# Value weights streamed in whole rows, and the segment's output turned into columns in two parts

## The chip, the cores and the metric

The kernel runs on one core of a Trainium2 chip. The metric is the device time of one execution in microseconds, as the median over several runs; lower is better. Four kinds of engine matter here: TensorE (PE, with PEld for its weight loads), VectorE (DVE), ScalarE (ACT) and GpSimd (POOL). SyncE (SP) issues most of the DMA transfers, and 16 DMA engines carry them.

## What is computed

The reference is a stack of four layers, A, B, A, B, each added to its input after a normalisation of the rows. Layer A is the one that matters here: attention in segments with a recurrent memory. The 2048 rows are cut into 64 segments of 32 rows. Eight rows of memory go in front of each segment, and the first eight rows of a segment's output are the memory of the next, so the segments can't run side by side.

```python
mem = mem0                                    # 8 rows of 640
for s in range(64):
    h = concatenate([mem, x[32*s:32*s+32]])   # 40 rows of 640
    q, k, v = h @ Wq, h @ Wk, h @ Wv          # 32 heads of 192
    p = softmax(where(mask, q @ k.T * scale, -1e9))
    o = (p @ v) @ Wo                          # back to 640 columns
    mem = o[:8]; outs.append(o[8:])
```

All inputs are in bf16. Wq, Wk and Wv are 640 x 6144 each, Wo is 6144 x 640. Layer B is a linear attention over all rows at once; the change doesn't touch it.

## The kernel before

Layer A has a part that is done for all segments at once (`A_pre`) and a chain over the 64 segments (`A_chain`), whose order on every engine is the order in which the program is written (`manual_schedule`). The last eight rows of each segment are projected in `A_pre`; the chain itself handles 32 rows: eight of memory and the segment's first 24. They lie in `hT` as columns: 128 partitions x 5 blocks x 32 columns, where block b holds every fifth one of the 640 features and the first eight columns of a block are the memory.

**A segment in rounds.** The 32 heads go in four rounds of eight. A round projects Q, K and V (`project`, L885: five blocks of four matmuls each), copies Q and K to SBUF on ACT (`to_raw`, L895), turns them on DVE (`to_rows`, L900 and L903 to L905), takes scores (`scores`, L922 and L927), exponentials and sums, weighs the values (`attend`, L935), and multiplies by the round's rows of Wo into one PSUM bank `W` (`wo_round`, L961), which gathers all four rounds. The order of the rounds turns round from segment to segment, so that the last round of one is the first of the next.

**Streamed weights.** Not all weights fit into SBUF. For each of Q, K and V, three of the five blocks (blocks 2, 3 and 4) of rounds 0 and 3 share a slot. In the first round of each segment `project` takes these three blocks first (its order of blocks is 2, 3, 4, 0, 1), and after each block `load_slot` issues on SP's queue the load of the last round's weights into that slot. Q comes as one DMA per block, whole rows of 3072 B in each of 128 partitions; K and V come as two DMAs per block, half rows of 1536 B. After the first round's `wo_round`, `load_wo` loads Wo's rows of the last round from `wo_rows` in six DMAs of 320 KB. So SP issues 21 weight loads in each segment, in this order: three of Q, six of K, six of V, six of Wo. A DMA on SP's queue waits for the DMA issued eight before it, since the framework has eight semaphores for this queue.

**The end of a segment.** After the last `wo_round` (with `keep_busy` and `fill`, which give PE matmuls and weight loads whose results nobody uses), the bank `W` holds the segment's output rows. DVE turns its 160 columns in 32 x 32 blocks into the tile `wt` (L1101) and copies eight columns of each of the five blocks into `hT` in bf16 (L1102). With that the next segment's first projection, Q of round 0, may start. After these, `keep_tail` (L949, L950) and `keep_rows` (L849, four ACT copies from `W`) put away what belongs to the output. In `W` an access by one engine waits for the other engines' earlier ones, reads included: that is how the framework orders the accesses to one PSUM bank.

Of the kernel before, what the change touches and what calls it, by code (L numbers as in the profile page):

```python
# [115 lines left out]
class Kernel:  # L116
# [456 lines left out]
    def layer_A(self, xn_dram, at_dram, li, x_raw=None):  # L573
        nc, tc = self.nc, self.tc
        KC, NSEG = self.KC, self.NSEG
        dram = self.dram
        NR = 4
        PW = 1536
        self.kqb_d = dram.tile([NSEG, P, NR, 192], BF16, name=f"kqb{li}")
        self.vb_d = dram.tile([NSEG, NR, 2, 8, 896], BF16, name=f"vb{li}")  # L580
        self.otb_d = dram.tile([NSEG, P, 384], BF16, name=f"otb{li}")
        wview = self.wview
        wov = self.A_Wo.rearrange("h d m -> (h d) m").rearrange("(c p) m -> p c m", p=P)
        low = self.view(0, LATE)
        at = LATE
        res, slot = {}, {}
        for r in (3, 2):
            for m in "KQV":
                for b in range(KC - (SLOTS[m] if r == 3 else 0)):
                    res[m, r, b] = low[:, len(res) * PW:len(res) * PW + PW]  # L590
        assert len(res) * PW * 2 == LATE
        for m, r, b in [(m, 0, b) for m in "KQV" for b in range(KC - SLOTS[m])] + \
                [(m, None, b) for m in "KQV" for b in range(KC - SLOTS[m], KC)] + [(m, 1, b) for m in "KQV" for b in range(KC)]:
            v = self.view(at, 2 * PW)
            at += 2 * PW
            if r is None:
                slot[m, b] = v
            else:
                res[m, r, b] = v
        holds = {}  # L600
        wo_mid = self.view(at, 24 * 1280)
        wo_end = self.view(at + 24 * 1280, 12 * 1280)
        assert at + 36 * 1280 == ARENA
        unread = set(res)

        def load_slot(m, r, b, whole=False):
            if holds.get((m, b)) != r:
                holds[m, b] = r
                w = PW if whole or m == "Q" else PW // 2
                for h in range(0, PW, w):  # L610
                    nc.sync.dma_start(out=slot[m, b][:, h:h + w], in_=wview[m][:, b, PW * r + h:PW * r + h + w])

        def load_matrix(m, r):
            for b in range(KC):
                if (m, r, b) in unread:
                    unread.remove((m, r, b))
                    nc.sync.dma_start(out=res[m, r, b], in_=wview[m][:, b, PW * r:PW * r + PW])
                elif (m, r, b) not in res:
                    load_slot(m, r, b, True)

        early = {(0, 5), (2, 4), (2, 5), (1, 0), (1, 1), (1, 2), (1, 3)}

        def load_wo(r, into=None, part=range(6)):
            t = into if into is not None else wo_end[:, :] if r in (0, 3) else wo_mid[:, 7680 * (r - 1):7680 * r]
            for k in part:
                tk = t[:, 1280 * k:1280 * k + 1280]
                if r in (0, 3):
                    self.last_load = nc.sync.dma_start(out=tk, in_=self.wo_rows[r // 3, :, 1280 * k:1280 * k + 1280])
                else:
                    nc.sync.dma_start(out=tk.rearrange("p (c m) -> p c m", m=640),  # L630
                                      in_=wov[:, 12 * r + 2 * k:12 * r + 2 * k + 2, :])

        def piece(m, r, b):
            assert (m, r, b) in res or holds[m, b] == r
            return res[m, r, b] if (m, r, b) in res else slot[m, b]

        def lay_out_wo():
            if li == 0:
                self.wo_rows = dram.tile([2, P, 7680], BF16, name="wo_rows")
                for i, r in enumerate((0, 3)):  # L640
                    nc.scalar.dma_start(out=self.wo_rows[i].rearrange("p (c m) -> p c m", m=640),
                                        in_=wov[:, 12 * r:12 * r + 12, :])

        def early_wo():
            for r in (0, 2, 1):
                load_wo(r, part=[k for k in range(6) if (r, k) in early])

        def late_wo(r):
            load_wo(r, part=[k for k in range(6) if (r, k) not in early])

        self.A_pre(xn_dram, li, load_matrix, piece, wo_mid, wo_end, lay_out_wo, early_wo, x_raw)
        self.A_chain(xn_dram, at_dram, li, load_slot, piece, load_wo, late_wo, wo_mid, wo_end, low)
        self.post_args = at_dram, wo_mid, wo_end, low

# [159 lines left out]
    def A_chain(self, xn_dram, at_dram, li, load_slot, piece, load_wo, late_wo, wo_mid, wo_end, low):  # L814
        nc, tc, KC, NSEG = self.nc, self.tc, self.KC, self.NSEG
        scale = float(self.Dh) ** -0.5
        NR = 4
        with tc.tile_pool(name=f"A{li}_ch", reuse_waits="tile", bufs=1) as sp, \
# [25 lines left out]
            def new_hT():  # L844
                return sp.tile([P, KC, 32], BF16, name="hT", tag="hT")
# [98 lines left out]
            def keep_tail(o, late=False):  # L944
                otb = sp.tile([P, 6, 16], BF16, name="otb", tag="otb", bufs=2)
                if late:
                    nc.vector.tensor_copy(out=otb[:, 0:3, :], in_=o[0][:, :, 64:80])
                else:
                    nc.scalar.activation(out=otb[:, 0:3, :], in_=o[0][:, :, 64:80], func=ACT.Copy)  # L949
                nc.vector.tensor_copy(out=otb[:, 3:6, :], in_=o[1][:, :, 64:80])  # L950
                return otb

            def store_tail(otb, s, r):
                nc.gpsimd.dma_start(out=self.otb_d[s, :, 96 * r:96 * r + 96], in_=otb[:, :, :].rearrange("p c t -> p (c t)"))  # L954
# [56 lines left out]
            hT = new_hT()  # L1011
            hx_transpose(hT, range(4))
            load_rows(1)
            for s in range(NSEG):
                W = pop.tile([P, 512], F32, name="ps_w", tag="w")
# [67 lines left out]
                if s + 1 < NSEG:  # L1083
                    hT = new_hT()
# [13 lines left out]
                fill(SEG_FILL)  # L1098
                if s + 1 < NSEG:
                    wt = sp.tile([P, KC, 32], F32, name="wt", tag="raw")  # L1100
                    nc.vector.transpose(out=wt[:, :, :], in_=W[:, 0:160].rearrange("p (j b) -> p b j", b=KC))  # L1101
                    nc.vector.tensor_copy(out=hT[:, :, 0:8], in_=wt[:, :, 0:8])  # L1102
                store_tail(keep_tail(o), s, order[L])
                keep_rows(W)
            store_rows(NSEG - 1)
# [66 lines left out]
```

## Time and profile before

| What | Value |
|---|---|
| Median of 6 runs | 3784.98 us (3777.33 to 3793.9) |
| The profiled execution | 3787.65 us, of which its span 3785.9 us |
| Mean granted TensorE clock | 0.976 |
| PE / PEld / DVE / ACT / POOL busy | 94% / 61% / 62% / 55% / 44% |
| Bytes read from HBM, written | 855.97 MB, 72.09 MB |
| First and last transpose at a segment's end (L1101), first layer A | 250.1 and about 1578 us |
| The same, second layer A | 2122.9 and 3444.9 us |

The busy share of PE is a mean over the span. In the rows of groups, the columns are: line, engine, operation, output and inputs with their shapes and the count; then busy time and the mean duration of one; then the engine's idle time just before these instructions and what ended it. In the timeline the columns are the start, the duration, the engine, the line, the operation, the tiles and the count, and in brackets the idle time before it with its releaser.

### The profile page before, as it was taken

To read this page: it belongs to the slowest core of one execution; us is meant where nothing else is said; L and a number is where in the kernel's file an instruction comes from. 1 tells how busy PE (TensorE), PEld (TensorE's weight loads), DVE (VectorE), ACT (ScalarE), POOL (GpSimd) and SP (SyncE) were. 2 spreads that over 40 slices of the span, in tenths; PEclk is the share of its full clock that TensorE was granted. 3 is DMA by queue.
4 is the path that set the end of the run, shared out by engine and by line. 5 is a ranking of instruction groups with operands and counts; after the bars stand their busy time and mean duration, and the time that the engine had idled before them with its cause. 6 is when DMAs were issued, how large, how long until landed. Compare 5 with 4: busy or idle time off the path is not lost. (4 is left out here: it accounts for less than half of the span.)

```text
span 3785.9 us, 169628 instructions
## 1 busy us (share of the span) xinstructions
PE 3546.5 (94%) x71080; PEld 2324.9 (61%) x71408; DVE 2329.1 (62%) x6038; ACT 2074.5 (55%) x5285; POOL 1671.4 (44%) x4367
## 2 busy tenths in 40 slices
PE   7889999999999999889899899999999999999898
PEld 5666666666666666545468566666666666665453
DVE  3546666666666666645643566666666666664565
ACT  2246666655666666536432566665666666664553
POOL 2435555545555555430242455545555555554300
PEclk9999999999999999989899999999999999999899
DMA  9788888887888888840377888888788888889100
GB/s 325 238 266 280 278 286 274 292 273 270 293 279 287 288 284 291 295 145 1 121 241 202 293 283 287 287 282 279 274 292 282 288 287 275 289 277 314 54 1 28
DMA packets 587913, 935.32 MB, mean 247 GB/s; under 512 B 147322, under 2 KB 402826, under 8 KB 587146
## 3 DMA queue, kind: packets, MB, share of 16 engines
q1 hardware_dynamic: 449194, 805.76, 61.2%
q0 software_dynamic: 68288, 88.95, 7.8%
q10 hardware_dynamic: 69664, 29.76, 3.0%
q8 instruction: 558, 9.14, 1.0%
q14 instruction: 209, 1.71, 0.1%
HBM read 855.97 MB, written 72.09 MB: 245 GB/s over the span
## 5 line engine op out<-in xcount | busy, mean ns | idle before, releaser
L885 PE MATMUL ps_qk<-arena,hT 128*32 128x384 bf16 x20480 | 1003.8, 328 | 28.5 <-DMA arena<-in_A_Wk_dram 6.9
L885 PEld LDWEIGHTS <-hT 128*32 128x32 bf16 x30720 | 741.2, 96 | 447.2 <-DVE hT L1102 33.5
L895 ACT ACTIVATE raw<-ps_qk 128x384 bf16<-128x384 f32 x1024 | 502.9, 491 | 445.8 <-PE ps_s L993 250.4
L961 PE MATMUL ps_w<-arena,OT 128*32 128x160 bf16 x24576 | 542.5, 234 | 27.0 <-DMA arena<-wo_rows 24.2
L868 POOL DMA_DIRECT2D Vp<-vb x512 | 259.5, 507 | 655.6 <-PE ps_o L935 452.2
L885 PE MATMUL ps_v<-arena,hT 128*32 128x384 bf16 x10240 | 536.3, 330 | 0.0
L961 PEld LDWEIGHTS <-OT 128*32 128x32 bf16 x24576 | 435.4, 97 | 120.9 <-issue 42.1
L900 DVE STREAM_TRANSPOSE KT<-raw 128x384 bf16<-128x384 bf16 x512 | 296.1, 578 | 201.5 <-ACT raw L895 197.5
L903 DVE STREAM_TRANSPOSE QT<-raw 128x256 bf16<-128x256 bf16 x512 | 228.0, 445 | 266.8 <-ACT raw L895 239.0
L856 POOL DMA_DIRECT2D kqb<-kqb x512 | 291.1, 569 | 165.7 <-POOL KT L864 148.4
L916 DVE CAST Vp<-ps_v 64x384 bf16<-64x384 f32 x512 | 286.1, 559 | 89.8 <-ACT Vp L914 75.6
L954 POOL DMA_DIRECT2D otb<-otb x512 | 283.5, 554 | 107.3 <-DVE otb L950 68.8
L914 ACT ACTIVATE Vp<-ps_v 64x384 bf16<-64x384 f32 x512 | 246.3, 481 | 144.6 <-PE ps_v L885 107.8
L941 DVE CAST OT<-ps_o 128x192 bf16<-128x192 f32 x512 | 183.1, 358 | 209.5 <-PE ps_o L935 192.8
L1000 DVE TENSOR_TENSOR E<-E,ps_s 80x320 bf16<-80x320 bf16 x512 | 247.4, 483 | 73.5 <-ACT ps_s L999 69.5
L935 PEld LDWEIGHTS <-Vp 80*128 80x128 bf16 x4096 | 181.5, 99 | 172.1 <-issue 124.0
L979 ACT ACTIVATE E<-ps_s 80x320 bf16<-80x320 f32 x512 | 221.9, 433 | 112.1 <-PE ps_s L927 99.6
L935 PE MATMUL ps_o<-E,Vp 80*128 80x80 bf16 x4096 | 234.0, 202 | 31.8 <-DMA Vp<-vb 8.6
L927 PE MATMUL ps_s<-QT,KT 128*80 128x80 bf16 (+1 forms) x3072 | 234.5, 214 | 24.0 <-DVE KT L900 15.3
L861 POOL COPY QT<-kqb 128x64 bf16<-128x64 bf16 x512 | 126.4, 247 | 281.6 <-PE ps_s L927 278.9
L927 PEld LDWEIGHTS <-KT 128*80 128x80 bf16 x3072 | 206.7, 120 | 55.6 <-issue 45.1
L940 ACT ACTIVATE OT<-ps_o 128x192 bf16<-128x192 f32 x512 | 167.9, 328 | 129.5 <-PE ps_o L935 129.3
(148 smaller groups left out, 5458.7 us busy)
## 6 DMA issues: line engine op xcount, KB each, us to landing
arena<-wo_rows SPq DMA_DIRECT2D x792, 320.0 KB, 6.0
arena<-in_A_Wq_dram SPq DMA_DIRECT2D x430, 384.0 KB, 4.6
arena<-in_A_Wk_dram SPq DMA_DIRECT2D x768, 192.0 KB, 4.7
arena<-in_A_Wv_dram SPq DMA_DIRECT2D x768, 192.0 KB, 5.4
kqb<-arena ACTq DMA_DIRECT2D x16, 1536.0 KB, 8.7
kqb<-kqb POOLq DMA_DIRECT2D x512, 48.0 KB, 5.0
arena<-in_A_Wk_dram SPq DMA_DIRECT2D x46, 384.0 KB, 7.1
arena<-in_A_Wv_dram SPq DMA_DIRECT2D x46, 384.0 KB, 7.8
```

Source lines behind the costliest of these rows:

```text
L856: nc.gpsimd.dma_start(out=kqb[:], in_=self.kqb_d[s, :, r, :])
L868: nc.gpsimd.dma_start(out=Vs[n % 2][64:80, :], in_=self.vb_d[s, r].rearrange("g t f -> (g t) f"))
L885: nc.tensor.matmul(o[32 * g:32 * g + 32, 0:384], lhsT=hT[:, b, :], rhs=rhs, start=(i == 0), stop=(i == KC - 1), tile_position=(0, 32 * g), ...
L895: nc.scalar.activation(out=raw[:], in_=ps[:, 0:384], func=ACT.Copy)
L900: nc.vector.transpose(out=KT[:, :, 0:64], in_=raw[:, :].rearrange("p (c j) -> p c j", j=64))
L914: nc.scalar.activation(out=o, in_=i, func=ACT.Copy)
L916: nc.vector.tensor_copy(out=o, in_=i)
L927: nc.tensor.matmul(S[0:80, c0:c0 + 80 * (q1 - q0)], lhsT=KT[:, 3 * x + i, :], rhs=QT[:, x, q0:q1, :], start=False, stop=(x == 1 and i == 2 ...
L935: nc.tensor.matmul(O[x][:, 80 * i:80 * i + 80], lhsT=Vs[n % 2][0:80, 448 * x + k:448 * x + k + 128], rhs=E[0:80, 160 * x + 80 * e:160 * x ...
L954: nc.gpsimd.dma_start(out=self.otb_d[s, :, 96 * r:96 * r + 96], in_=otb[:, :, :].rearrange("p c t -> p (c t)"))
L961: nc.tensor.matmul(W[32 * g:32 * g + 32, 0:160], lhsT=OT[:, c, q:q + 32], rhs=w[:, 640 * i + 160 * g:640 * i + 160 * g + 160], start=(firs ...
L1000: nc.vector.tensor_tensor(out=E[0:80, 0:320], in0=E[0:80, 0:320], in1=rc, op=ALU.mult)
```

## The change

Two edits. `load_slot` now loads V in one DMA per block with whole rows of 3072 B, as it does Q; K stays in halves. At the segment's end, DVE turns and copies blocks 2, 3 and 4 first (96 columns), and then blocks 0 and 1 (64 columns): four instructions in place of two.

```diff
         def load_slot(m, r, b, whole=False):
             if holds.get((m, b)) != r:
                 holds[m, b] = r
-                w = PW if whole or m == "Q" else PW // 2
+                w = PW if whole or m in "QV" else PW // 2
                 for h in range(0, PW, w):
                     nc.sync.dma_start(out=slot[m, b][:, h:h + w], in_=wview[m][:, b, PW * r + h:PW * r + h + w])
...
                 if s + 1 < NSEG:
                     wt = sp.tile([P, KC, 32], F32, name="wt", tag="raw")
-                    nc.vector.transpose(out=wt[:, :, :], in_=W[:, 0:160].rearrange("p (j b) -> p b j", b=KC))
-                    nc.vector.tensor_copy(out=hT[:, :, 0:8], in_=wt[:, :, 0:8])
+                    for b0, b1 in ((2, 5), (0, 2)):
+                        nc.vector.transpose(out=wt[:, b0:b1, :], in_=W[:, 0:160].rearrange("p (j b) -> p b j", b=KC)[:, b0:b1, :])
+                        nc.vector.tensor_copy(out=hT[:, b0:b1, 0:8], in_=wt[:, b0:b1, 0:8])
                 store_tail(keep_tail(o), s, order[L])
                 keep_rows(W)
```

## The prediction

> **What bounds the kernel now.** I read the page first: PE is busy nearly everywhere, but the DMA engines are too, and the bulk of it is SP's queue, q1.
>
> ```profile
> PE 3546.5 (94%) x71080; PEld 2324.9 (61%) x71408; DVE 2329.1 (62%) x6038; ACT 2074.5 (55%) x5285; POOL 1671.4 (44%) x4367
> ...
> DMA  9788888887888888840377888888788888889100
> ...
> q1 hardware_dynamic: 449194, 805.76, 61.2%
> ...
> L961 PE MATMUL ps_w<-arena,OT 128*32 128x160 bf16 x24576 | 542.5, 234 | 27.0 <-DMA arena<-wo_rows 24.2
> ...
> arena<-in_A_Wq_dram SPq DMA_DIRECT2D x430, 384.0 KB, 4.6
> ...
> arena<-in_A_Wv_dram SPq DMA_DIRECT2D x768, 192.0 KB, 5.4
> ```
>
> So I cut one segment (1006.08 to 1027.68, from L1101 to L1101) into windows. Columns: stretch, length, busy time of PE, PEld, DVE, ACT, POOL, clock, DMA share, GB/s.
>
> ```profile
> 1006.08:1008.00 1.92, 1.77 (x37) 1.16 (x40) 0.64 (x3) 1.43 (x5) 0.00 (x0) 1.00 0.05 11
> 1008.00:1016.00 8.00, 7.91 (x180) 4.82 (x172) 6.14 (x16) 5.23 (x14) 4.90 (x14) 1.00 1.00 349
> 1016.00:1025.00 9.00, 8.84 (x256) 5.95 (x244) 6.01 (x16) 5.95 (x16) 4.96 (x14) 1.00 0.97 335
> 1025.00:1027.68 2.68, 2.11 (x63) 1.67 (x64) 1.59 (x5) 0.54 (x2) 1.61 (x3) 1.00 0.32 95
> ```
>
> For 17 us the DMA engines are full; at both ends they are idle. Setting the record of landings against the starts of L1101 shows what that means. The 124 intervals between two L1101 (62 in each layer A) sum to 2649.8 us: the shortest is 20.84, the median 21.21. In 63 of them the next L1101 comes 0.41 us (within 0.025) after the segment's last Wo piece lands: they hold 36.7 us over 20.85 each. In the others PE's own work is the bound, plus scattered stalls. Two chains run side by side, then: PE's order, about 20.85 us, and the transfers, which start behind the first Q matmuls and end with Wo.
>
> The segment's end, in the timeline:
>
> ```profile
> 1006.08 0.35 DVE L1101 STREAM_TRANSPOSE wt<-ps_w 128x160 f32<-128x160 f32 x1
> ...
> 1006.46 1.21 ACT L849 ACTIVATE Vp<-ps_w 32x160 bf16<-32x160 f32 x4 [0.76 <-DVE wt L1101]
> 1006.47 0.18 DVE L1102 CAST hT<-wt 128x40 bf16<-128x40 f32 x1
> 1006.57 0.19 DVE L950 CAST otb<-ps_o 128x48 bf16<-128x48 f32 x1
> ...
> 1006.70 1.81 PE L885 MATMUL ps_qk<-arena,hT 128*32 128x384 bf16 x40 [0.15 <-DVE hT L1102]
> ...
> 1007.75 0.49 ACT L895 ACTIVATE raw<-ps_qk 128x384 bf16<-128x384 f32 x1
> ...
> 1008.27 0.45 DVE L903 STREAM_TRANSPOSE QT<-raw 128x256 bf16<-128x256 bf16 x1 [1.52 <-ACT raw L895]
> ...
> 1009.28 0.58 DVE L900 STREAM_TRANSPOSE KT<-raw 128x384 bf16<-128x384 bf16 x1
> ```
>
> PE waits for the copy; ACT's `keep_rows` waits for the transpose, a mere read of the same bank, and only 0.07 us lie between its end and Q's copy.
>
> **Whole V rows.** 768 V packets of 1536 B per segment become 384 of 3072 B. By the packet records in the chain, a 1536 B packet of q1 takes 70.1 ns on average (median 65), so V costs 768 x 70.1 = 53.8 us of one DMA engine. A 3072 B packet has a median of 121 and, in Q's loads, a mean of 146; but Q's first ones start on idle engines (193 ns in the third microsecond, 129 in the fourth, 145 and 131 after). V runs on full engines, where 1536 B lies 8% over its median, so I take 121 x 1.08 = 130.5: 50.1 us. Over 16 engines that saves 0.23 us of the transfer chain; bounds: 0.46 at 121 ns, a loss of 0.15 at 146. The three DMAs fewer save 48 semaphore packets of 9 ns, 0.03 us, left out. SP issues V three DMAs sooner (the second half of the last block now waits for a landing until 9.6 us behind L1101, Wo's first piece until 10.5); that gains nothing by itself, since the engines are full anyway and Wo's first piece waits for PE's reads of its buffer too. V lands by about 14.8 us behind L1101 and is used from 15.9 on, so a whole piece is in time.
>
> **Turning in two parts.** The rows of DVE's transposes (578 ns at 384 columns, 445 at 256) give 1.04 ns a column. Ninety-six columns take 350 - 64 x 1.04 = 283 ns, 64 take 250; of 182 ns the copy of 24 elements keeps 165, that of 16 some 155 (slope of 1.1 ns from the 48 and 192 column copies, 201 and 358 ns). From the first transpose's start, with gaps of 0.034 behind a dependence and 0.053 to PE: first copy 0.317 to 0.482, PE at 0.537 in place of 0.62, so **0.084 us sooner**. The second transpose needs nothing from the copy; L950 starts 0.10 us behind L1102's start, so I start it 0.085 behind the first copy's: 0.40 to 0.65; second copy 0.69 to 0.84. PE reaches block 0 after twelve matmuls of 41 ns at 1.03; covered.
>
> What pays is ACT. `keep_rows` now waits for the second transpose: 0.685 in place of 0.383, ending at 1.90. Q's copy then starts at 1.91 in place of 1.67 (+0.24). K's copy waits for PE until 2.46 anyway and is not late. DVE's three Q turns end at 3.41 (now 3.17), K's at 4.02 (now 3.77); the first score weights need K's 0.05 later, at 4.07, where PE now loads them at 4.02 and would at 3.93. The score matmul starts 0.03 later: at 4.10, now 4.15. So of 0.084 us PE keeps about **0.04**. If the second transpose waits for the copy's end, all of this shifts by 0.11 and PE loses 0.07; if nothing is late, it gains 0.08. DVE's `keep_tail` copy comes 0.4 us later, at about 1.0; its store leaves POOL at 3.06 and hides that.
>
> The Trainium skill, "VectorE: DVE Perf Modes", § The DRAIN you can't avoid, says the next operation can't start until the pipe is empty: by it PE would lose the 0.07, and the sum below would be 7 us in place of 18. Its later section on two Vector instructions with no wait lets one that isn't held start earlier, as L950 does here. The same skill, "DMA: Bandwidth & Descriptors", § Queues, rings and completion order, has each engine drain a whole packet of several descriptors of one queue before the next: by that rule POOL's small loads would wait behind longer V packets, which speaks against whole rows.
>
> **The sum.** The transfers start sooner too, since the first Q load follows the first Q matmuls: 0.23 + 0.084 = 0.31 us for intervals that end by Wo, each taken down to no less than PE's 20.81. 44 of the 63 have 0.31 to give; interval by interval, with the other stalls kept, it is 15.0 us. The other 61 give 0.04 each, 2.5. With the two boundaries outside these intervals: 18 us. The profiled execution (3787.65; span 3785.9 and 1.75 around it) lies 2.7 above the median, so 3769.7 there and **3767** as a median. Ends of the bounds: 0.46 + 0.08 with PE's 0.08 give 28 us; a V loss of 0.15 with PE's loss of 0.07 makes it 9 us slower.
>
> **Rivals.** Nothing to measure: V's packets cost as much a byte as before (the mean of 146 speaks for it, the median against), and the late `keep_rows` eats the rest; 1 to 2 us, or 8 from the earlier start alone: about 3783.
>
> Slower: the first projection waits for the second copy, because the wait for `hT` covers the tile and not its blocks. Place: L885 behind L1102. Price: PE starts at 0.89 in place of 0.62, 0.27 x 126 = 34 us, less V's 11: 3808. It decides as soon as block 2's wait covers columns 0 to 63. Against it: Wo's six pieces lie in one tile and PE waits for each by itself.
>
> Also slower: POOL's `Vp` loads, 4.6 us from issue to landing already, come behind longer packets. PE waits 8.6 us for them now; a V DMA has eight packets on each engine, 8 x (130 - 70) = 0.48 us at most. In some 25 segments that would cost 12 us, on all 124 nearly 60.
>
> **Chances.** Forecast 0.55 (own range 3756 to 3774), nothing to measure 0.29, the tile's wait 0.10, POOL's loads 0.06. What a measurement can tell from no change is about 0.3%, 11 us; the runs before spread over 17 us. Faster 0.55, same 0.29, slower 0.16. The range takes in the bounds, 3757 to 3794, and 2 us for the median's scatter below: 3755 to 3794; the tile's wait stays out.
>
> **What would show it.** L1101 and L1102 x252, the first transpose at 0.28 us, PE's first Q matmul 0.54 behind it; Wv x430 at 384 KB and no half rows; V's packets near 130 ns and the last Wo piece 0.3 us sooner; `keep_rows` 0.3 later behind the first transpose, with a small PE wait for KT at L927. I am wrong if that wait exceeds 0.1 us in most segments, if L885 waits till the second copy, or if V's packets cost 140 ns.

## The result and the profile after

The changed kernel takes 3774.29 us (median of 34 runs, 3761.9 to 3780.27), the kernel before 3777.93 in 68 runs beside it. The two medians lie 3.6 us apart; the ratio is 0.9986 [0.9979, 0.9993], which is 5.3 us, between 2.6 and 7.9. The sign is the forecast's; the size is under a third of its 18 us and below the 0.3% that the prediction took for what can be told from no change. The profiled execution took 3775.63 us, its span 3773.9. That of before, 3787.65, turns out to lie 10 us above the median of 68.

The page of the kernel after, in the parts shown of before (engines, DMA share, queues, one group, DMA issues):

```profile
PE 3549.1 (94%) x71080; PEld 2321.6 (62%) x71408; DVE 2361.7 (63%) x6290; ACT 2074.6 (55%) x5285; POOL 1671.4 (44%) x4367
...
DMA  9788887878888787840377878888788888889100
...
q1 hardware_dynamic: 393898, 805.73, 60.2%
...
q8 instruction: 558, 9.14, 1.0%
...
L961 PE MATMUL ps_w<-arena,OT 128*32 128x160 bf16 x24576 | 541.3, 234 | 27.2 <-issue 20.7
...
arena<-wo_rows SPq DMA_DIRECT2D x792, 320.0 KB, 6.7
...
arena<-in_A_Wv_dram SPq DMA_DIRECT2D x430, 384.0 KB, 6.4
```

The line to stop at is L961. PE idles 27.2 us before Wo's matmuls, as it did (27.0). Before, 24.2 of that ended with a landing of `wo_rows`; now 20.7 end with "issue": PE waited for nothing that the profile shows. One stall has gone and another stands in its place.

The segment's end, timeline of the kernel after:

```profile
1016.67 0.28 DVE L1102 STREAM_TRANSPOSE wt<-ps_w 128x96 f32<-128x96 f32 x1
...
1016.99 0.17 DVE L1103 CAST hT<-wt 128x24 bf16<-128x24 f32 x1
1017.08 0.23 DVE L1102 STREAM_TRANSPOSE wt<-ps_w 128x64 f32<-128x64 f32 x1
...
1017.22 1.81 PE L885 MATMUL ps_qk<-arena,hT 128*32 128x384 bf16 x40
1017.35 0.17 DVE L1103 CAST hT<-wt 128x16 bf16<-128x16 f32 x1
1017.39 1.21 ACT L849 ACTIVATE Vp<-ps_w 32x160 bf16<-32x160 f32 x4 [1.83 <-DVE wt L1102]
...
1018.63 1.00 ACT L895 ACTIVATE raw<-ps_qk 128x384 bf16<-128x384 f32 x2
...
1019.15 0.45 DVE L903 STREAM_TRANSPOSE QT<-raw 128x256 bf16<-128x256 bf16 x1 [1.52 <-ACT raw L895]
...
1020.15 0.58 DVE L900 STREAM_TRANSPOSE KT<-raw 128x384 bf16<-128x384 bf16 x1
...
1020.85 0.26 PEld L927 LDWEIGHTS <-KT 128*80 128x80 bf16 x4 [0.16 <-issue]
```

PE starts 0.55 us behind the first transpose, while the second copy is still to come: `hT` is waited for by its blocks. `keep_rows` (L849) starts after the second transpose, Q's copy (L895) follows at 1.96, and the score weights at the end come late: the 0.16 us of idle time before them stand in 124 of the 126 segments, where before there was none (but in two). Medians over the 126 ends of segments (in the last row over the 124 intervals between two ends), in us behind the first transpose's start:

| Step | before | predicted | after |
|---|---|---|---|
| first Q matmul | 0.622 | 0.537 | 0.546 |
| `keep_rows` starts | 0.383 | 0.685 | 0.726 |
| Q's copy starts | 1.669 | 1.91 | 1.964 |
| K's turn on DVE ends | 3.772 | 4.02 | 4.067 |
| first score matmul | 4.152 | 4.10 | 4.213 |
| last Wo piece lands | 20.70 | 20.39 | 20.36 |

**Where the time went.** The 124 intervals between two segments sum to 2640.4 us (2649.8 before): 9.4 less, where 17.5 were predicted. I compared the mean lengths of the runs of matmuls between them, times 124. The last Wo round, which waits for Wo, loses 32.2 us. The stretch from the turning to the scores gains 7.6. The third Wo round gains 31.0, of which 15.6 come back in the idle matmuls behind it, which are followed by another wait anyway. The sum of these is -9.2.

The third Wo round, timeline of PE alone after:

```profile
458.70 0.51 PE L885 MATMUL ps_v<-arena,hT 128*32 128x384 bf16 x8
459.03 0.30 PE L961 MATMUL ps_w<-arena,OT 128*32 128x160 bf16 x5
460.69 0.94 PE L961 MATMUL ps_w<-arena,OT 128*32 128x160 bf16 x43 [1.35 <-issue]
```

Five matmuls run, then nothing for 1.35 us, then the other 43. The stall is always between the fifth and the sixth, with no semaphore in it. The records say what is there: PE has 71080 + 71408 = 142,488 matmuls and weight loads, and 404 semaphore and drain instructions that the page leaves out. That makes 142,892, and 142,892 / 256 = 558.2, against 558 packets on q8, the queue "instruction", of 9.14 MB / 558 = 16.4 KB each. PE's program is itself streamed in, 256 instructions to a packet, over the same 16 DMA engines. Nearly every segment (122 of 124) has exactly 1024 PE instructions (three of them semaphore instructions), four blocks, so the places where PE moves on to a new block are the same in all: instruction 193 of each 256, by the trace's records. When PE moves on to a block, the next one seems to be asked for: the first packet of a segment, on idle engines, starts 0.65 us behind such a place. The third is asked for while V's and Wo's loads run. It used to start 2.17 us after PE had passed the place before (about 11.8 us behind the transpose), at 14.1; now 3.32 us after, at 15.1. It takes 1.04 us, and PE goes on a median of 1.37 us after it ends: 17.5, just when PE gets there. Before, 13 of 124 segments stalled there, for 3.9 us in all; after, 59, for 33.5 us.

### The profile page after: what moved, and what is told of

Its sections match the earlier page's. It is cut to its first block, busy times and chain, and to the rows that moved or that the text cites. A ratio compares the mean times of both kernels' runs of the same rounds, so it can differ in the third digit from the quotient of the medians.

```text
span 3773.9 us, 169108 instructions
## 1 busy us (share of the span) xinstructions
PE 3549.1 (94%) x71080; PEld 2321.6 (62%) x71408; DVE 2361.7 (63%) x6290; ACT 2074.6 (55%) x5285; POOL 1671.4 (44%) x4367
## 3 DMA queue, kind: packets, MB, share of 16 engines
q1 hardware_dynamic: 393898, 805.73, 60.2%
q8 instruction: 558, 9.14, 1.0%
## 5 line engine op out<-in xcount | busy, mean ns | idle before, releaser
L895 ACT ACTIVATE raw<-ps_qk 128x384 bf16<-128x384 f32 x1024 | 503.1, 491 | 391.5 <-PE ps_s L993 250.4
L961 PE MATMUL ps_w<-arena,OT 128*32 128x160 bf16 x24576 | 541.3, 234 | 27.2 <-issue 20.7
L961 PEld LDWEIGHTS <-OT 128*32 128x32 bf16 x24576 | 434.7, 97 | 120.3 <-issue 43.0
L927 PE MATMUL ps_s<-QT,KT 128*80 128x80 bf16 (+1 forms) x3072 | 234.0, 213 | 22.0 <-DVE KT L900 13.1
L849 ACT ACTIVATE Vp<-ps_w 32x160 bf16<-32x160 f32 x512 | 150.7, 294 | 174.2 <-DVE wt L1102 155.1
L927 PEld LDWEIGHTS <-KT 128*80 128x80 bf16 x3072 | 195.8, 119 | 71.0 <-issue 61.8
```

Source lines behind the costliest of these rows:

```text
L895: nc.scalar.activation(out=raw[:], in_=ps[:, 0:384], func=ACT.Copy)
L927: nc.tensor.matmul(S[0:80, c0:c0 + 80 * (q1 - q0)], lhsT=KT[:, 3 * x + i, :], rhs=QT[:, x, q0:q1, :], start=False, stop=(x == 1 and i == 2 ...
L961: nc.tensor.matmul(W[32 * g:32 * g + 32, 0:160], lhsT=OT[:, c, q:q + 32], rhs=w[:, 640 * i + 160 * g:640 * i + 160 * g + 160], start=(firs ...
```

## The experiments

The theory: both parts work, but V's longer packets hold up PE's instruction blocks, which takes back much of what the earlier Wo gives, and the late `keep_rows` turns the earlier first projection into a later score matmul. The rivals: the new stall comes from the turning; or one of the two parts is simply worth nothing. Ratios are to the kernel before, run beside it on the same chip.

**V in whole rows alone.**

```diff
-                w = PW if whole or m == "Q" else PW // 2
+                w = PW if whole or m in "QV" else PW // 2
```

> V in whole rows alone, the segment's output turned in one piece as before. Theory A (V's rows shorten the transfers, but PE's instruction blocks, one packet of 16 KB each, now come later behind them; the turning in two parts costs PE time): the waits for Wo's last piece fall as in the changed kernel (last round's excess from 39 to about 8 us), the stall at the sixth matmul of the third Wo round stays as there (50 to 60 of 124 segments, about 30 us), the shortest interval is again 20.84 us; 8 to 13 us faster than the kernel before. Rival B (the instruction stall comes with the two-part turning, which shifts the work): fewer than 15 segments stall there, 20 us or more faster. Rival C (whole rows bring nothing, the turning is what gained): within 3 us of the kernel before.

Measured: 3772.47 us, 0.9978 [0.9961, 0.9994]. Its groups by shape:

```profile
L961 PE MATMUL ps_w<-arena,OT 128*32 128x160 bf16 x24576 | 543.2, 234 | 28.6 <-issue 18.3 <-DMA arena<-wo_rows 8.1
```

Both sides of the trade are in this one line, with the turning untouched: the wait for Wo falls to 8.1 and "issue" rises to 18.3. The trace has 54 segments stalled at the sixth matmul, 30.8 us. The score matmul is at 4.152, as before. The stall belongs to V's rows.

**The turning alone.** The transposes and copies in two parts, V in halves.

```diff
-                w = PW if whole or m in "QV" else PW // 2
+                w = PW if whole or m == "Q" else PW // 2
```

(against the changed kernel)

> The turning in two parts alone, V in half rows as before. Theory A: first score matmul 0.06 us later behind the first transpose (4.21 for 4.15), shortest interval 20.91 us in place of 20.84; intervals that end by Wo begin 0.075 us sooner; few instruction stalls (15 segments or fewer); in all between 2 us faster and 6 us slower. Rival B: 50 or more segments stall at the sixth matmul of the third Wo round, and it is 10 us slower or more. Rival C: 5 to 10 us faster.

Measured: 3776.38 us, 0.9994 [0.9979, 1.0008], no difference that this resolves. The same group:

```profile
L961 PE MATMUL ps_w<-arena,OT 128*32 128x160 bf16 x24576 | 537.6, 234 | 22.5 <-DMA arena<-wo_rows 20.5 <-issue 0.3
```

No stall of the new kind (4 segments, 1.2 us), Wo's wait as before. The score matmul is at 4.213, so the loss of 0.061 us on PE comes from here alone.

**`keep_rows` on DVE.** If the four copies on ACT are what makes the scores late, DVE can take them, in the changed kernel:

```diff
-                    nc.scalar.activation(out=orow[:, 160 * g:160 * g + 160], in_=W[32 * g:32 * g + 32, 0:160], func=ACT.Copy)
+                    nc.vector.tensor_copy(out=orow[:, 160 * g:160 * g + 160], in_=W[32 * g:32 * g + 32, 0:160])
```

> The changed kernel with the four copies of keep_rows on DVE in place of ACT. Theory A (the 0.06 us that PE loses come from ACT: keep_rows waits for the second transpose and holds up Q's copy): Q's copy starts near 1.59 us behind the first transpose in place of 1.96, DVE turns K by 3.9, the score matmul comes at 4.08 in place of 4.21, the shortest interval falls from 20.91 to about 20.77; 8 to 12 us faster than the changed kernel, 13 to 18 faster than before. Rival (DVE itself is what holds K's turn): the score matmul stays at 4.15 to 4.25, no gain over the changed kernel.

Measured: 3761.8 us, 0.9952 [0.9938, 0.9967]. Q's copy starts at 1.596, K's turn ends at 3.936, the score matmul comes at 4.083, and the shortest interval falls from 20.91 to 20.773.

```profile
L849 DVE CAST Vp<-ps_w 32x160 bf16<-32x160 f32 x512 | 165.3, 323 | 11.2 <-PE ps_w L961 2.1
```

A copy costs DVE 323 ns where it cost ACT 294, yet DVE has the time and needs no hand-off behind its own transposes. So ACT's queue, not the transposes, kept the gain of the two parts from PE: 0.13 us a segment. The fetch stall stays (61 segments, 29.1 us).

**V in whole rows, two DMAs of 64 partitions each.** The question was whether the block's packet waits for the rest of one DMA or for a certain number of packets.

```diff
+                if m == "V" and not whole:
+                    for p in (0, 64):
+                        nc.sync.dma_start(out=slot[m, b][p:p + 64, :], in_=wview[m][p:p + 64, b, PW * r:PW * r + PW])
+                    return
```

(against the kernel before)

> The kernel before with V in whole rows of 3072 B, but two DMAs of 64 partitions for each block, so that each DMA has four packets on each engine in place of eight. Theory A1 (the instruction block waits for one DMA's group of packets on its engine, about 1.0 us for eight of 3072 B and 0.5 for four): the third block's packet starts near 14.1 us as before and not 15.1, 20 segments or fewer stall for it, Wo's last piece lands 0.2 to 0.3 us sooner than before; 12 to 18 us faster than before. Rival A2 (the length of the single packets, or the longer queue in bytes, delays the blocks): the block's packet starts at 14.8 or later, some 50 segments stall, time as with whole rows in one DMA.

Measured: 4029.34 us, 1.0663 [1.0637, 1.0688]. From its page:

```profile
q1 hardware_dynamic: 400042, 805.76, 64.1%
...
L965 PE MATMUL ps_w<-arena,OT 128*32 128x160 bf16 x24576 | 592.3, 235 | 182.7 <-DMA arena<-wo_rows 127.1
```

Nearly as many packets as after, and as many bytes, but the share of engine time rises from 60.2% to 64.1% of a longer span: V's packets take 185 to 208 ns (by the microsecond in which they start) in place of 130. The experiment was meant to change the grouping alone and changed the price, so it doesn't settle its question; that the block came no sooner (at 15.6 us) with only four V packets a DMA on each engine, and that 78 segments stalled at the sixth matmul, speaks against the first reading. What it shows by the way is that the transfers are a bound: the last Wo piece lands at 22.64, and the median interval goes to 23.11.

**The blocks shifted.** If the stall is the fetch, its place must follow the instruction count. `FILL` holds idle weight loads that run once, in the first segment of each layer A; 90 fewer in the first layer move every boundary 90 instructions later in the segment. Three kernels have it: the changed one, the one with `keep_rows` on DVE, and the kernel before as control.

```diff
-FILL = {0: 122, 2: 78}
+FILL = {0: 32, 2: 78}
```

> The changed kernel with 90 fewer of the idle weight loads that run once ahead of the first layer A's chain (32 for 122), so that every boundary between two blocks of 256 PE instructions comes 90 instructions later in the segment in both layers: the third one leaves the third Wo round and falls among the idle matmuls behind it. Theory A (the stall at the sixth matmul of that round is the wait for an instruction block): the stall at that matmul is gone, 5 or fewer segments; the shortest interval stays 20.91; the total is 8 to 20 us below the changed kernel, since idle matmuls hide part of the wait, unless another boundary now stalls. Rival (the stall belongs to that matmul, by its weights, its bank or its engine): it stays in 50 to 60 segments, and the time is that of the changed kernel.

> Both together: the changed kernel with keep_rows on DVE and the boundaries 90 instructions later. Theory A: shortest interval 20.77 us, no stall at the sixth matmul of the third Wo round; 25 to 35 us faster than the kernel before, about 3750 us where that is 3778. If the stall only moves to another place, the time is that of the changed kernel with keep_rows on DVE, some 17 us faster than before.

> The kernel before with the boundaries 90 instructions later: the control. With V in half rows the third block came early enough (13 of 124 segments stalled, 3.9 us in all), so theory A expects no more than 4 us of gain and, where another boundary now stalls, a few us of loss. Rival (the shift itself is worth the time, whatever V does): as large a gain as the shift brings to the changed kernel.

Measured: 3942.83 us, 1.0423 [1.0395, 1.0452]; 3924.88, 1.0394 [1.0355, 1.0433]; the control 3847.8, 1.0183 [1.0156, 1.021]. I had the place right and the sign of the time wrong. From the groups by shape, the idle matmuls behind the third Wo round, in the first kernel and then in the control:

```profile
L968 PE MATMUL ps_idle<-arena,ident 128*128 128x192 bf16 x512 | 86.4, 252 | 163.4 <-issue 163.3
```

```profile
L968 PE MATMUL ps_idle<-arena,ident 128*128 128x192 bf16 x512 | 84.8, 253 | 85.9 <-issue 84.9
```

And the timeline of PE in the first:

```profile
1006.30 1.00 PE L961 MATMUL ps_w<-arena,OT 128*32 128x160 bf16 x48
1007.23 0.34 PE L968 MATMUL ps_idle<-arena,ident 128*128 128x192 bf16 x2
1009.43 0.34 PE L968 MATMUL ps_idle<-arena,ident 128*128 128x192 bf16 x2 [1.86 <-issue]
```

The Wo round is now whole, with no stall at its sixth matmul in any segment, and PE stops two idle matmuls later: still instruction 193 of 256. That makes the fetch the cause. Why it got worse: the place at which a block is asked for moved from 11.8 to 14.3 us, 2.5 later, but the place where it is needed moved only from 0.30 us into the Wo round (459.03 to 459.33) to 1.27 us into it (1006.30 to 1007.57), 1.0 later. The margin shrank by 1.5 us, and 121 stalls there make 182 us, 1.5 us each. (The second block now stalls too, in about 50 segments, for 24 us.) The control has the same loss of margin, but its third block starts 0.8 us sooner: 113 stalls, 103 us. So the same boundaries cost 66 us with half rows and 165 with whole ones, and the boundaries of the kernel before lie well by comparison.

**K in whole rows too.**

```diff
-                w = PW if whole or m in "QV" else PW // 2
+                w = PW
```

> The changed kernel with K in whole rows too (15 weight loads in each segment). Theory A: the transfers get shorter again by about 0.2 us, Wo's last waits fall under 5 us, but the second instruction block, fetched while K's packets run, starts later than the 9.0 us of now, near 10, and since PE reaches it at 11.8 to 11.9 behind the first transpose, a new stall of 0.1 to 0.6 us appears there in many segments; the third block no earlier than 15. Time from 3 us faster to 10 us slower than the changed kernel. Rival (the blocks wait for V alone, by its place in the segment): the second block as now, no stall there, 4 to 8 us faster than the changed kernel.

Measured: 3850.5 us, 1.0182 [1.0155, 1.0208].

```profile
L961 PE MATMUL ps_w<-arena,OT 128*32 128x160 bf16 x24576 | 553.2, 235 | 60.0 <-issue 56.0 <-DMA arena<-wo_rows 3.9
```

Wo's wait is nearly gone (3.9 us), as more whole rows should make it, and the fetch costs more than all of that: the second block of a segment, which falls into K's loads, now starts 2.95 us behind its place (1.98 after) and makes 81 stalls of 46 us in the projections; the third starts 3.79 behind and stalls over 100 segments. The mechanism was expected, not a size of 70 us.

**Fewer whole rows of V**, in the kernel with `keep_rows` on DVE: the last block in halves, then only the first block whole, then none.

```diff
-                w = PW if whole or m in "QV" else PW // 2
+                w = PW if whole or m == "Q" or (m == "V" and b < KC - 1) else PW // 2
```

> The changed kernel with keep_rows on DVE, and V's last streamed block (block 4) in half rows again, blocks 2 and 3 whole. Theory A (the third instruction block, asked for at 11.8 us, waits for the packets that are queued then, about sixteen of V's, so the length of the packets queued at that time decides): half packets ahead of it, so its packet starts 2.3 to 2.8 us after the boundary in place of 3.2; 20 to 40 of 124 segments stall at index 193 in place of 61, 8 to 18 us in all in place of 29; 4 to 10 us faster than keep_rows on DVE with V all whole. Rival (the stall hangs on V's bytes in the queue, not on the length of the packets): as many stalls, no gain.

```diff
-                w = PW if whole or m in "QV" else PW // 2
+                w = PW if whole or m == "Q" or (m == "V" and b == KC - 3) else PW // 2
```

> As the run with only the last block in half rows, but blocks 3 and 4 both in half rows, block 2 whole. Theory A: the third block's packet starts 2.1 to 2.4 us after the boundary, 15 segments or fewer stall, 5 us or less in all; Wo's last piece a little later than with V all whole; 5 to 12 us faster than keep_rows on DVE with V all whole. Rival: as many stalls as there.

```diff
-                w = PW if whole or m in "QV" else PW // 2
+                w = PW if whole or m == "Q" else PW // 2
```

> The two-part turning with keep_rows on DVE and V in half rows throughout: the change's second edit alone, with its cost on ACT taken away. Theory A: shortest interval 20.77 us, 15 or fewer stalls at index 193, Wo's last round waits as in the kernel before (about 35 us); 6 to 12 us faster than the kernel before, so that V in whole rows is still worth 5 to 10 us on top. Rival (whole rows lose more by the instruction blocks than they gain): as fast as, or faster than, the same kernel with V whole, 17 us or more below the kernel before.

| `keep_rows` on DVE, whole V blocks | us | ratio | third block starts | stalled at the sixth matmul | 124 intervals |
|---|---|---|---|---|---|
| three | 3761.80 | 0.9952 [0.9938, 0.9967] | 15.0 | 61, 29.1 us | 2631.0 |
| two | 3758.38 | 0.9945 [0.9926, 0.9964] | 14.97 | 58, 26.4 us | 2629.6 |
| one | 3750.84 | 0.9933 [0.991, 0.9956] | 14.56 | 26, 11.6 us | 2617.5 |
| none | 3770.58 | 0.9986 [0.9969, 1.0003] | 13.7 | 5, 1.9 us | 2638.0 |

The same group with one whole block and with none:

```profile
L961 PE MATMUL ps_w<-arena,OT 128*32 128x160 bf16 x24576 | 539.1, 234 | 18.6 <-DMA arena<-wo_rows 10.7 <-issue 5.8
```

```profile
L961 PE MATMUL ps_w<-arena,OT 128*32 128x160 bf16 x24576 | 539.0, 235 | 24.4 <-DMA arena<-wo_rows 22.4 <-issue 0.8
```

Taking the last block back to halves did nothing that shows: a miss, and what the rival had said. The third block starts 3.24 us behind its place, as with three whole blocks (3.28), though the transfers of that time are shorter (97 ns on average for 115). So their length alone is not what holds it up. With one whole block the fetch starts 0.4 us sooner than with three and more than half of the stalls go, while Wo's last piece still lands at 20.36 and its wait is half of what it is with none. I had expected no more than 15 stalled segments. This version has the lowest time of all and is faster than both kernels; its interval overlaps those of the two rows above it, so the order among the three is not settled by these runs; their distance to "none" is.

## Why the prediction was right and wrong

**Right.** V's packets cost 129.6 ns where I took 130.5, and Wo's last piece lands 0.35 us sooner (0.31). The first part of the turning is turned and copied in the time given, to 0.01 us. The second transpose started 0.09 us after the first copy, which lasts 0.175: it needs nothing from it. The Trainium skill, "VectorE: DVE Perf Modes", § The DRAIN you can't avoid, has the next instruction wait for the empty pipe, but adds that one which isn't held starts earlier; this pair agrees with the addition. That PE lost about what the first rule would have cost it (0.061 for 0.07) is chance: the loss came from another place. The tile's wait did not come. POOL's `Vp` loads were not held up: from issue to landing they take 4.5 us (4.6 before), and PE waits 3.6 us for them in all (8.6 before). The chain from `keep_rows` over Q's copy and the turns to the score weights is the one that moved.

That the time lies in the range of 3755 to 3794 says little. The kernel before lies in it too (3777.93), and 3767 was reckoned from six runs whose median was 7 us above that of the 68. The gain lies between the forecast's 18 us and the rival "nothing to measure" (1 to 2, or 8), and of that rival's two conditions one held: the late `keep_rows` cost PE what the turning gave, but V's packets did get cheaper by the byte.

**First step that failed: "So of 0.084 us PE keeps about 0.04".** PE lost 0.061, and the sign that I had set for being wrong came true: the weights at L927 waited more than 0.1 us in most segments (0.16 us of idle time in 124 of 126). Two hand-offs were sized by the wrong rows. `keep_rows` starts 0.083 us behind the second transpose, where I took the 0.034 of before (its first copy now carries three waits in place of two; that this is the reason isn't shown); and the score weights are loaded 0.115 behind K's turn, where I took 0.05, the gap from a copy of `hT` to its small weights. The right row was in the trace of before all along: in a segment's last round, L927 follows K's turn by 0.115. The copies took 0.175, not 0.165 and 0.155. The score matmul at 4.213 in place of 4.10 makes 0.11 us in every interval that PE bounds, 14 us if all were. The turning alone and `keep_rows` on DVE show the place.

**Second: a term left out of "The sum".** I took the transfers as a chain that ends with Wo and asked only whom else on POOL's queue it would delay. PE's own instructions ride on the same engines. Of the earlier issue of V I had written "that gains nothing by itself"; what it does to whoever else has to get through was left out. The delay of one block from 2.17 to 3.32 us put 31.0 us into the third Wo round, 15.4 of them net. V's rows alone, the shifted blocks and the kernel with whole K rows show it.

I weighed a rule for this and gave it to POOL's queue alone. The Trainium skill, "DMA: Bandwidth & Descriptors", § Queues, rings and completion order, says that an engine finishes a packet of some 9 to 17 descriptors from one ring before it turns to the next. Counted from the place where the third block seems to be asked for to its packet's start, more passes here: each engine starts some 22 of q1's transfers before (12.7 half rows of V and 9.7 rows of Wo) and 26 after (4.9 whole rows of V and 21.4 of Wo). So of the extra 1.15 us the longer rows of V, by this count, make some 4.9 x 60 ns = 0.3, an estimate. The rest goes with Wo's pieces, which SP now issues sooner (the fifth at 11.90 us in place of 13.16). That V's whole rows delay the block is shown; why it waits for just so many transfers stays open, for within the kernel before the delay hardly depends on how many of Wo's pieces are out (2.0, 2.3 and 2.1 us with one, two and three).

**Third: the base.** The profiled execution lay 10 us above the median of the later 68 runs. Its 36.7 us of waiting for Wo, from which I took 15.0 of the gain, was thus more than usual. This I have only as a difference between runs. And the 63 intervals were too few: the landings that I used tell the last piece in 93 of the 124 alone. Read from that piece's semaphore in all of them, 79 intervals end 0.41 us behind it and hold 45.2 us, which by the same working would have made the 15.0 about 19.

Put together, 15.0 + 2.5 us were expected in the intervals. The wait for Wo gave more, 32.2, presumably because the fetch makes PE itself late and so covers some of it: where the fetch stalls are few, one whole block of V against none takes the wait of the last Wo round from 35.4 to 20.1 us, 15.3, near the term of the sum, though with one whole block and not three. Of the 32.2 go 7.6 for the turning and 15.4 for the fetch; 9.2 are left. That is for this pair of traces, of which the one of before was long; the many runs put the gain at 5.3.

## What to carry to other kernels

Where an engine stops at the same place of its program again and again and the profile names no releaser, count its instructions: a block of program may be late behind bulk transfers, and a change that makes the transfers cheaper or issues them sooner is then paid for by an engine that moves no data. When a step is split, follow the reader that has to wait for its last part, and who is queued behind that reader: here four copies on ACT that nobody needs soon cost more than the split saved. And where two chains run side by side, try to move both: V's whole rows gave 0.22% alone, the turning with `keep_rows` on DVE 0.14% (not told from nothing: its interval ends at 1.0003), both together 0.48%. That they give more together than one by one is not shown; the intervals are too wide.

## What the runs showed of the hardware

PE's program comes in blocks of 256 instructions as 16 KB packets of 1.04 us on the engines that carry data. Counted from the place where PE moves on to the block before, a block's packet starts 0.65 us later on idle engines. On full ones it depends on the place, and is later with whole rows at each of three: 2.0 and 2.9 us at 6.9 us behind the transpose (K in half and in whole rows), 0.95 and 2.1 at 9.6 (V, in the kernels with shifted blocks), 2.2 and 3.3 at 11.8 (V). PE goes on 1.37 us after the packet's end. A shift by 90 instructions, with no work changed inside the segment, made the kernel with half rows 1.8% slower and put the one with whole rows 4.2% behind the kernel before.

V's packets of 3072 B took 130 ns when a DMA covered 128 partitions and 196 when it covered 64. The copy of 24 elements and that of 16 cost the same, by the groups by shape of the kernel after (columns: busy time and mean ns of one, then idle time before):

```profile
L1103 DVE CAST hT<-wt 128x24 bf16<-128x24 f32 x126 | 22.2, 176 | 4.4
L1103 DVE CAST hT<-wt 128x16 bf16<-128x16 f32 x126 | 22.0, 175 | 4.4
```
